# The last of 32 attention pairs turned in 32-row blocks, a one-column function at each change of ScalarE's table, and a new order of issue

## Chip, core and metric

One core of a Trainium2 chip runs the whole kernel. The metric is device time in microseconds (us) from launch to end, the median over several executions. Five engines run side by side, each with its own queue of instructions: TensorE (PE in the profile, with its weight loads as PEld), VectorE (DVE), ScalarE (ACT), GpSimd (POOL) and SyncE (SP), which only issues DMA transfers here.

## What is computed

Thresholded attention over 8 batches of 8 heads (576 tokens, head size 64), and behind it a gated MLP with a spatial gate. Cut to what matters:

```python
scores = scale * q @ k.T                                # 64 heads, 576 x 576
keep   = scores >= max(scores) - tau
attn   = where(keep, exp(scores - max(scores)), 0)
attn   = attn / (sum(attn) + 1e-9)
x      = heads_side_by_side(attn @ v)                   # (8, 576, 512)
h      = gelu_tanh(x @ w_in)                            # 512 -> 1024
u, v   = h[:, :512], h[:, 512:]
v_n    = (v - mean(v)) / sqrt(var(v) + 1e-6) * g_ln
v_s    = w_sg @ v_n + b_sg                              # mixes the 576 tokens
out    = x + (u * v_s) @ w_out
```

## The kernel before

**Attention.** The 64 heads are worked off as 32 pairs, four to a batch. A pair has nine score tiles: four of 128 query rows for each of its two heads, and one tile in which the last 64 rows of both heads share the partitions. A tile goes through a fixed sequence: scores on TensorE (L546, split into a rounded part and a remainder; L524 for the first four pairs), row maximum on VectorE (`nm`, L555), the threshold on GpSimd (`thr`, L561), the exponential on ScalarE (L582), and on VectorE the selection with the row sum (L589).

What then happens to the exponentials has two forms. In pairs 4 to 30 (`by_rows` is true) VectorE turns each tile in blocks of 32 x 32 (`turn_blocks`, L599), and TensorE multiplies them with the values in 288 small products of 32 rows (`turned_values`, L755), in up to six pieces. The values come in a layout that is repeated four times over the partitions, in four loads. The inverse row sums leave as one small transpose (`turn_rows`, L242), are copied by ScalarE (`take_rows`, L655), written to DRAM by three small DMAs (`put_rows`) and read back, spread over the partitions, by two (`get_rows`). VectorE then scales the result (`scale_turned`, L762, two halves).

In pairs 0 to 3 and in pair 31, the last, the form is the older one: TensorE turns the exponentials with whole 128 x 128 transposes (L242), ScalarE copies them from PSUM (L715, L730), and the value product (`values`, L741) follows in two parts, tokens 0 to 255 and 256 to 575. The inverse sums are repeated by GpSimd, turned by TensorE and copied by ScalarE, without DRAM.

Either way ScalarE rounds the result to `xh` (L780) and GpSimd takes the remainder `xl` (L785). These two are the input of the MLP.

**MLP.** A batch's MLP is cut into units of 8 to 14 products (L849): `v` units (moving width 512), `u` units, gate units `y` and output units `o` (width 288, or 256 and 320 in the last batch). A `v` unit runs over the four pairs of its batch; the last four of its twelve products need the batch's fourth pair. `v` and `u` units pass through gelu on ScalarE (L838). ScalarE holds one table of functions at a time: exp and gelu stand in two tables, and each change costs an ACT_TABLE_LOAD.

**Order.** Every step is first put into a list, `plan`. A table of numbers that is packed as text (`ORDER`) says in which order the steps are issued to the engines, and a second one (`FIRST_BANKS`) which of the eight PSUM banks each step takes. Each engine works its own part of that order strictly in turn:

```python
    def issue(plan):
        with tc.manual_schedule():
            for i in order:
                plan[i].fn()
```

The tail of the program is the MLP of the last batch: nothing of its `v` and `u` units can be finished before pair 31 is.

Of the kernel before, what the change touches and what calls it, by code (L numbers as in the profile page):

```python
# [22 lines left out]
P = 128  # L23
# [14 lines left out]
    "mK)W70_1gFy$8G1J1PU%|V;ChK6psNPywt2jHbcFf4nEN;GbJyM;l-yi$J`zN^6)s-UTzw(N;V%g3tJK&)1R0B3zxpl2tkBx6FLH^p~>)akE+*ZvSc$8"
    "=2NMU6De$>h|k7(5jjzjKQ74K(6)3)B1@>@Q@w%)b3q!5m#Tgy!}vEQZ9Z-YBcm9ejVXrLIU~i#t@_L*ErrWlTvT6p+#p5>Q)7x%0k^^9WfSO+&9LYxp"
    "TRo}m_;qI0UCBgO@q`&)pqVtNj1V@irhN0jdxs(jdD9Glk|llsw{oNITgbykItw1Om~7DHiBa+L*x?xDKqU8Vd0b##>wY|EB;HlPeGDu@FzHtc+kwE>J"  # L40
    "#CZM$~Yp^NF?1af!?^93nL4mkQJEdH{2%a!Us1)bMF0gn=;K8*VsR)C9+5I2tptYM2e-Rghss;uFlZD>+L23gsjyeoEVygR%A%@g$g({HmWN)fa}tlj#"
    "$2OB}zT+s73-*NVY0k42Cqs@<nZq6FG9$(I%T_|3XE;}rSl!Lk?>zv5?>@QPvz7xfzj!mzL!VnS@f&&9+O=Z-%jNUqC%@mVo==LQ*gKR3%2{Jeuwzi1u"
    "d8fRKK!iG66W|S%-mqyWZlxU4fay#solc4&AEoQ{e)es)K;GPwZ*=MFf@f&1wLw?$BXAmPidF<Y#LqOr-Q$8w!r((ivfy@m~P&VgRgffC)eDLfmf;>?j"
    "f*7-Om^;RwB6#u(W)weFOoYOtKiqBwT56tCc!rsG7Nx?=kY(M7htb4SCK;3o=Zg51xNkE(JSGmtOp4#M!f+ZWggTXs#0u7!IWwom0^&k`?p~CGVmgp`h"
    "9r|3$%sC@QiO9}_guy-Kk-bBYzgy5it(OkOoN(9HIgApkO}a-aCw#(Gs}u(CWbRD7OJ^s+HD&Wvu|=>e!_VXG#KT_tCLW%NJQQ_7h;uANiwU5)1$R*g~"
    "Z=hpA4tQbI%G`(#+a13PdP~ylG-pn*6sv<%)5%Y(h~qVn7zrVo*4#30oS`SVBd`;HVKS>iETSCY(Qwn<il<xIS$wF2cjpm}wIL<%3*~n5{tZ6S1xd!=x"
    "Fd&5hv*`@>s;s+x!k!4Z5Q61ObzUn(NgB&jV|2ABLt<5?p#EX37#12VS`{1VE>m^gEa84>=&Cr2XaZ{O4@AEsPR#3u=yhMF0uCSakEh=fm5!y;#h+u@d"
    "2*lbpq6dW6O91b<gkZ5M#B4(Ltw9OnB5g>W^f=I!aFew-j+(;&JL)%!qglkiie<Q`zh>zK#ta1dyZT#{?5*~q3R#fEH;EtG14I;Q3!jr)5Qf`FuB#Ue?"
    "dnU7H=uCjS*NBl-Gar)RHM}c}QjsJPH!(1xj8&)9xaYA-Ces|JRnl3TAx1;vj4@MID*O@385c$=uNc9nz}N0*EWA+7EIk7dmlv8wwNtJATd62VUY1&0N"
    "uipKS1Z5OtsEFb#WO@Doke9XxA2PM(NGlDg&<F~m8HmBio7mF*RZ0H7FMP#T~s%+s<k^m6Vau^z01mMh6~6lYzhtZZq==neF?*%3*L1$h4)sGaz=(2;u"  # L50
    "ot<+g|w?PTiyv1<b<XqiB%|RpC}Q_eB;8^DG>47#Iq3z(80TgOtH)lM(E(8_F>=NhZkrP_D^E*)P*(bhW*hN~SyRglCQl-o@GwKG_X5V&PsSo=I+u=xj"
    "vz)D4Uhm(h7_lJKav{YOW5k1{|oo~(NKP1CBkdxKym7)qXr@PA_HX0zg?a0;kkQW9}<mu(x4^!H<})b1rE+<na>IW;eBdnj$M@V7T8+O~21&3IV7U7(b"
    "jhoAQEpl!<LsjQvxzu&cq{0*5U1b@g7il7#NyiP4seg^rL%|||b@y^20KL+gJw+-_YM|d1TH*{zQRa1u?9#rni0(-fO^eI#2%Y%03kzjNMSTd{9j(LV0"
    ")0LY}4Q^_QYKcBYzzLowziTP5{1B9zQ|lU{2Ub-;y0b!#=}_Zn(eB$8Ogr8&wT^Z<KD>zpsS7$@bCN)f><1zzyQ8gE@VaXH$^McqT}Z<>Pj^NjxffbVl"
    "ag2Fxsci8j5m_B*5<h~PbVDfeKDhncsjWvgWYP?dR<K+FWfazm814~h#VOJ@WiFm1)~-Hw{b2~9iO?Udjiy7j!tVjkuFE&{?@5%9DFw8tn-?7&YBU`^F"
    "lXRe@9v04o#k*x4wtFctU_Qcu&ZS*U0hyG;+1ektBeWZ&FSd{0wkMQzsw+@|`DZGHgqh8hVobX(^;*lw;@JJK=caOGVKC&52+Ir|kN1jIE-3^R;nTu5T"
    "NYVynB*{Ro`_P}=EgY4Bf%NbtynKYC=ibO>6lQji29<QL{P6n=C%rOpcWRt>+u%w7kx))&a&>$VlH73eY64G)6ti|MOp-iRfEEz{-CcMhDjbMlFg@0|k"
    "Z@vfbS>nd2&pc0hG8-wbXjQ{?PItAno_4YtnPWMt>v3@x<8e*<CEl*hR@)8m`ch!y9mN%cP|Li4a>s$5DgIA8tJ=nb>E_U|EA&}PqTm<`)7dHSDz&G<?"
    "J>1ih`EltR0E^$G8`%A1d&3WpEqe?;anD~qA3l9?>_30#Esx(Zo)#={cs@P@&PO1LyfFXm7e76G6l4p?H{uF5mkjhp>JOI`O@OaR)0K%Zycrx&*5eaRb"
    "uV(kW=ogaOejgOeQa5elHMTauL;awn>HLGewwUmpn&$eyYFyV-P#N8Tb!GJ#BUp^0{CE`Mh2{&w{i|GcqRjOz%xzI2<+3?<G0BThkJAY`1y7KT{$!uU@"  # L60
    "5@+-y9lzD2dd(6uoic7b+qf1F&z@u6tqKR8;y#mm{BlPd|1m!#q6jfu&$Oozx2_ww>>l0##$boUZS={pay1XXApfVutd4w_(3QUJ-`((ZW8#sFq;N$0V"
    "m>LPV7BE0_}VOGz(gCUA!1xyjn=r0fJa1#09BSUXc*50F@&>VN?dI&K;LKRJ7c?8+gT0BHafhwWtaevcj}xa&P;m!{}SYwNB_U-uzFB5P`j0#JEVDJ07"
# [37 lines left out]
FIRST_BANKS = (  # L100
    "c-l3RO9I3&2ttkVbN?I9gLJyEO+^Gv1W(pPoV*o7$Q!3Jc<VGy<N#_iIbFg6Juw?+g;AmcY@S<frX1H^D(iI4DM8LS2XjTgmU(8c`n_&XMbTxdDXAg0g"
    "y}R60s5xJl5w+gfKfbZ<pZB*b+E|zlCu_@k}a1}EtjQ_gcdQ7_6>s-<-%=RUG#g2EAdzo-mm`j=j<nww(Hp(9cxepN&s?(JeMwL)Bw=1fwz?G<3w3}!p"
    "UuX>?%Qw+j!z5Ta^7b5N}qk-rMyrvr&jRvk=uhz5d%?!_+M=LJD;wMho$Dw9NblCgn<#ZFxFx%<^!an|&0om1^sTN30>$dIxJVd~Mo+i3p1kE)I~@NF+"
    "n@bw6(>T;N!g<g<88#}A9<2vh"
# [1060 lines left out]
```

## Time and profile before

| | |
|---|---|
| median of 3 runs | 906.46 us (905.97 to 910.84) |
| profiled execution, its own time | 908.68 us |
| its span, first to last instruction | 906.9 us |
| TensorE busy | 852.6 us, 94% |
| VectorE busy | 702.9 us, 78% |
| ScalarE busy | 601.4 us, 66% |
| GpSimd busy | 588.3 us, 65% |
| ACT_TABLE_LOAD | 100, 1283 ns each |

The profiled execution took 2.22 us more than the median, and 1.78 us of it lie outside the span. Busy TensorE time counts overlapping products once, so that the rest of the span, 54.3 us, is time without any product in flight.

### The profile page before, as it was taken

What the parts mean: (1) busy time and instruction counts of PE and PEld (TensorE: products, weight loads), DVE (VectorE), ACT (ScalarE), POOL (GpSimd) and SP (SyncE); (2) the same over time, 40 slices, a digit from 0 to 9 for tenths busy, and PEclk for the clock granted to TensorE, in tenths of its full rate; (3) what the DMA queues carried; (4) which work ended last, traced back from release to release, by engine and by line L of the source; (5) the groups of instructions that cost most, each with busy time, mean ns of one, the idle gap of its engine ahead of it and who ended that gap; (6) DMA issues with size and microseconds to landing.
All of it is one profiled execution on the core that took longest, in us unless ns stands there. A gap on an engine that the chain in (4) does not pass through costs nothing.

```text
span 906.9 us, 30418 instructions
## 1 busy us (share of the span) xinstructions
PE 852.6 (94%) x12440; PEld 752.9 (83%) x12440; DVE 702.9 (78%) x1436; ACT 601.4 (66%) x985; POOL 588.3 (65%) x973
## 2 busy tenths in 40 slices
...
GB/s 213 228 84 99 118 86 84 170 184 130 127 107 143 156 168 125 157 170 170 116 102 138 142 169 144 90 175 146 134 136 151 97 177 110 162 86 23 27 8 59
DMA packets 71998, 115.79 MB, mean 128 GB/s; under 512 B 10033, under 2 KB 32049, under 8 KB 71858
## 3 DMA queue, kind: packets, MB, share of 16 engines
...
q14 instruction: 42, 0.34, 0.1%
...
## 4 chain that ended last, share of the span: by engine, by line
PE 45%; DVE 18%; POOL 12%; ACT 10%; issue 8%; DMA 5%; SPq 2%; POOLq 0%; DVEq 0%; ACTq 0%
PE all_banks L849 26%; PE all_banks L546 8%; DVE nm L555 6%; DVE p L589 5%; PE all_banks L755 4%; DVE turned L599 4%; ACT p L582 3%; PE all_banks L242 2%; POOL ot L1056 2%; PE all_banks L741 2%; POOL vv L950 2%; PE all_banks L524 1%; POOL klz L448 1%; ACT L838 1%; POOL z L963 1%
## 5 line engine op out<-in xcount | busy, mean ns | idle before, releaser
L582 ACT ACTIVATE p<-all_banks,nm 128x576 f32<-128x576 f32 x256 | 184.5, 741 | 111.4 <-DVE nm L555 109.8
L589 DVE SCALAR_TENSOR_TENSOR p<-all_banks,nm,p 128x576 f32<-128x576 f32 x256 | 202.4, 808 | 51.7 <-ACT p L582 30.8
L555 DVE TENSOR_REDUCE nm<-all_banks 128x1 f32<-128x576 f32 x288 | 207.7, 742 | 34.6 <-PE all_banks L546 23.9
L546 PE MATMUL all_banks<-ks,qst 128*128 128x288 f32 x560 | 166.1, 316 | 19.1 <-DVE p L589 7.4
L599 DVE STREAM_TRANSPOSE turned<-p 128x576 f32<-128x576 f32 x216 | 159.1, 755 | 3.3 <-PE all_banks L755 3.2
L546 PE MATMUL all_banks<-klz,qst 128*128 128x288 f32 x560 | 156.8, 298 | 1.6 <-POOL klz L448 1.5
L561 POOL TENSOR_TENSOR nm<-columns,nm 128x1 f32<-128x1 f32 x288 | 53.3, 192 | 150.9 <-DVE nm L555 130.5
L755 PE MATMUL all_banks<-turned,v 32*64 32x144 f32 x7776 | 142.3, 286 | 3.8 <-issue 2.5
L755 PEld LDWEIGHTS all_banks<-turned,v 32*64 32x64 f32 x7776 | 123.1, 130 | 17.6 <-issue 13.8
L546 PEld LDWEIGHTS all_banks<-ks,qst 128*128 128x128 f32 x560 | 106.4, 190 | 36.6 <-DVE p L589 16.8
L849 PE MATMUL all_banks<-wsh,z 128*128 128x288 f32 (+2 forms) x512 | 114.1, 302 | 3.2 <-DVE pm L589 2.6
L546 PEld LDWEIGHTS all_banks<-klz,qst 128*128 128x128 f32 x560 | 106.8, 191 | 4.9 <-POOL klz L448 3.0
L849 PEld LDWEIGHTS all_banks<-wsh,z 128*128 128x128 f32 x512 | 86.5, 192 | 5.5 <-DVE pm L589 3.2
L448 POOL TENSOR_TENSOR klz<-rk,khi 64x576 fp32r<-64x576 f32 (+1 forms) x56 | 80.0, 1428 | 14.9 <-PE all_banks L546 5.6
L849 PE MATMUL all_banks<-gh,woh 128*128 128x288 f32 (+2 forms) x256 | 76.9, 303 | 2.7 <-DVE ir L762 1.3
L849 PE MATMUL all_banks<-xh,wih 128*128 128x288 f32 (+2 forms) x256 | 75.2, 298 | 2.1 <-DVE p L589 2.1
L849 PE MATMUL all_banks<-xh,wil 128*128 128x288 f32 (+2 forms) x256 | 74.1, 296 | 2.6 <-issue 2.6
L849 PE MATMUL all_banks<-wsl,z 128*128 128x288 f32 (+2 forms) x256 | 75.8, 300 | 0.0
L849 PE MATMUL all_banks<-gh,wol 128*128 128x288 f32 (+2 forms) x256 | 75.3, 297 | 0.0
L849 PE MATMUL all_banks<-xl,wih 128*128 128x288 f32 (+2 forms) x256 | 74.6, 296 | 0.0
L849 PE MATMUL all_banks<-gl,woh 128*128 128x288 f32 (+1 forms) x240 | 71.4, 299 | 1.8 <-issue 1.8
L838 ACT ACT_TABLE_LOAD x50 | 64.2, 1283 | 12.4 <-PE all_banks L849 10.8
...
## 6 DMA issues: line engine op xcount, KB each, us to landing
...
```

Of the source, the lines that this page charges most:

```text
L242: nc.tensor.transpose(out, x, ident_r.bitcast(F32))
L448: nc.gpsimd.tensor_tensor(klz[h][rows, 0:w], st["k"][rows, o:o + w], st["kh"][rows, o:o + w], ALU.subtract)
L546: nc.tensor.matmul(sc[:, a, 0:HALF], w, x, start=(j == 0), stop=(j == len(terms) - 1))
L555: nc.vector.tensor_reduce(nmax, st["s", h, i][:, :, 0:HALF], AX.XY, ALU.max, negate=True)
L561: nc.gpsimd.tensor_tensor(thr, toff, st["nm", h, i], ALU.subtract)
L582: nc.scalar.activation(target(h, i), st["s", h, i][:, :, 0:HALF], AF.Exp, bias=st["nm", h, i])
L589: nc.vector.scalar_tensor_tensor(dst, st["s", h, i][:, :, 0:HALF], st["thr", h, i], dst, ALU.is_ge, ALU.mult, accum_out=st["l"][:, c:c + 1])
L599: nc.vector.transpose(st["turned"][:, :, o:o + Q], st["p", i][:, c0:c0 + S].rearrange("p (k x) -> p k x", x=Q))
L741: nc.tensor.matmul(acc[h * D:(h + 1) * D, 0:w], st["v"][:, o:o + D], unit(h, a)[:, kt, 0:w] if kt < NM else tail_unit(a)[:, 0:w], start=(k ...
L755: nc.tensor.matmul(st["accs"][g // 2][hs, g % 2, 0:W], st["v"][rows, o:o + D], st["turned"][rows, k, h * W:(h + 1) * W], start=(k == 0), s ...
L838: put("gelu", end, lambda: nc.scalar.activation(tile_of(), acc_of(), AF.Gelu_apprx_tanh))
L849: nc.tensor.matmul(st["acc"], *term(j), start=(j == 0), stop=(j == n - 1))
```

## The change

Three things change. First, pair 31 takes the block-turned form of the pairs in front of it; the host side lays out its queries, keys and values accordingly. Second, wherever the order goes over from exp to gelu or back, a ScalarE function of one column (on a constant, into a column that nobody reads) is issued just ahead of the first function of the new kind. Third, the table `ORDER` and the table `FIRST_BANKS` are new.

```diff
 ORDER = (
-    "c-mE133wCL7M?R{?o65{Z7HQKZCSctX$uGxq#*bN!6%zg5J8`Spnxdiz96`M`rMw%Q)J%+!39*1@(=_!6j@3UC`)%*3bX}E(lp6T(%g6My)$V|!(`^(v"
+    "c-m!H31Ade((bP(^Li#TnVf{&90`G3gi}O7@IVlOH7trQt{@1=t|wmjdoAdyxazO02!<QnT}2KNqH=gcI2E}AxgaDYBq8Tq-AShZcXZFh{c}urzgP8D)"
...
     columns = cpool.tile([P, 4], F32, name="columns")
+    spare = cpool.tile([P, 1], F32, name="spare")
...
-        parts = SPLIT if whole_s or n == B * HP - 1 else ((0, S),)
+        parts = SPLIT if whole_s else ((0, S),)
         by_rows = len(parts) == 1
...
-    issue(plan)
+    issue(plan, {kind: partial(nc.scalar.activation, spare, mhalf, f)
+                 for kind, f in (("exp", AF.Exp), ("gelu", AF.Gelu_apprx_tanh))})
...
-    pairs = [divmod(n, h // 2) for n in range(WHOLE_SCORES, b * h // 2 - 1)]
+    pairs = [divmod(n, h // 2) for n in range(WHOLE_SCORES, b * h // 2)]
...
-    def issue(plan):
+    def issue(plan, tables):
+        ready = None
         with tc.manual_schedule():
             for i in order:
+                kind = plan[i].kind
+                if kind in tables and kind != ready:
+                    if ready:
+                        tables[kind]()
+                    ready = kind
                 plan[i].fn()
```

Over the whole program TensorE keeps its 32 pairs' scores and all MLP products. The program before holds 100 table loads, 50 ahead of exp and 50 ahead of gelu; the changed one holds 90, one at the start and 89 ahead of the one-column functions.

**TensorE at the last pair, before.** These rows stand where pair 31's product with the values is made. The tiles `p` and `pm` hold exponentials, `ir` and `l` inverse sums, `pt` the turned exponentials, `rv` the values; rows on `wol` and `woh` are `o` units of batch 6. Row by row, a count at the end means so many products of that kind in turn.

```order
L849 MATMUL all_banks<-gh_0_1_12135,wol_123 128x288
L242 MATMUL all_banks<-ident_r,p_2_12519 128x128 x5
L242 MATMUL all_banks<-ident_r,p_3_12573 128x128 x5
L242 MATMUL all_banks<-ident_r,pm 128x128 x4
L242 MATMUL all_banks<-ident_r,p_3_12573 128x128 x4
L724 MATMUL all_banks<-both,pm 128x64
L242 MATMUL all_banks<-ident_r,ir_12583 128x128 x2
L242 MATMUL all_banks<-ident_r,l_12140 128x128
L741 MATMUL all_banks<-pt_0_12498,rv_2576 64x256 x10
L741 MATMUL all_banks<-pt_1_12569,rv_2576 64x320 x10
L849 MATMUL all_banks<-gh_1_0_12621,woh_116 128x288
L849 MATMUL all_banks<-gl_1_0_12627,woh_116 128x288
```

Eighteen whole transposes, the inverse sums and both parts of the value product stand in one block; the `o` units of batch 6 come behind it.

**TensorE at the last pair, changed.** The same place. `turned` holds the exponentials after VectorE's block turns, `v_31` the repeated values; a count of 96 on such a row stands for two thirds of the 288 small products.

```order
L242 MATMUL all_banks<-ident_r,ir_12644 65x128
L849 MATMUL all_banks<-gh_1_0_12662,woh_117 128x288
L849 MATMUL all_banks<-gl_1_0_12690,woh_117 128x288
L849 MATMUL all_banks<-gh_1_0_12662,wol_121 128x288
L849 MATMUL all_banks<-gh_1_0_12662,woh_118 128x288
L849 MATMUL all_banks<-gh_1_0_12662,woh_117 128x288
L849 MATMUL all_banks<-gl_1_0_12690,woh_117 128x288
L849 MATMUL all_banks<-gh_1_0_12662,wol_121 128x288
L849 MATMUL all_banks<-gh_1_0_12662,woh_118 128x288
L755 MATMUL all_banks<-turned_12522,v_31_12580 64x144 x96
```

The one transpose of the inverse sums comes first, eight products of `o` units follow, then two thirds of the small products. Another 20 products of `o` units stand between these and the last third, and 16 more behind it.

**ScalarE at a change of table, before.** This is the second half of batch 0's `u` units (`uu0_1`), with what each row waits for in brackets.

```order
L582 ACTIVATE p6_0_1854<-all_banks_93,nm6_1_0_1861 128x576 [waits DVE_49]
L838 ACT_TABLE_LOAD [waits PE_49]
L838 ACTIVATE uu0_1_0_1897<-all_banks_93 128x288 [waits Activation_49]
L838 ACTIVATE uu0_1_1_1899<-all_banks_93 128x288 [waits Pool_49]
L1053 ACTIVATE ot0_0_0_1901<-all_banks_93 128x288 [waits PE_49]
L655 ACTIVATE ir5_1895<-all_banks_93 9x128 [waits PE_49]
L838 ACTIVATE uu0_1_2_1909<-all_banks_93 128x288
L582 ACT_TABLE_LOAD
L582 ACTIVATE p6_1_1920<-all_banks_93,nm6_0_1_1918 128x576 [waits DVE_49]
```

The load ahead of gelu carries the wait for TensorE, the load ahead of exp carries none.

**ScalarE at the same place, changed.**

```order
L582 ACTIVATE p6_0_1848<-all_banks_93,nm6_0_0_1846 128x576 [waits DVE_49]
L1164 ACT_TABLE_LOAD
L1164 ACTIVATE spare_106<-columns_105 128x1 [waits Activation_49]
L838 ACTIVATE uu0_1_2_1900<-all_banks_93 128x288 [waits Pool_49]
L838 ACTIVATE uu0_1_1_1902<-all_banks_93 128x288 [waits PE_49,Pool_49]
L439 ACTIVATE qhi7_1904<-rq7_1730 128x640 [waits DMAHW4_49,DMAHW5_49,DMAHW3_49,DMAHW2_49]
L838 ACTIVATE uu0_1_0_1906<-all_banks_93 128x288
L1053 ACTIVATE ot0_0_0_1908<-all_banks_93 128x288 [waits PE_49]
L655 ACTIVATE ir5_1876<-all_banks_93 9x128 [waits DMAHW1_49,PE_49]
L1164 ACT_TABLE_LOAD
L1164 ACTIVATE spare_106<-columns_105 128x1 [waits Activation_49]
L582 ACTIVATE p6_1_1930<-all_banks_93,nm6_0_1_1927 128x576 [waits DVE_49]
```

Each load now stands ahead of a one-column function that waits for nothing but an earlier one of its kind; the wait for the MLP products has gone to the gelu behind it.

**VectorE at the last pair, changed.** Names as above; `uu` are gate products of batch 6 and `nm` row maxima.

```order
L555 TENSOR_REDUCE nm_0_3_12609<-all_banks 128x1
L555 TENSOR_REDUCE nm_1_3_12617<-all_banks 128x1
L589 SCALAR_TENSOR_TENSOR p_3_12611,l_12223<-all_banks,nm_1_3_12617,p_3_12611 128x576
L599 STREAM_TRANSPOSE turned_12522<-p_2_12541 128x18x32
L589 SCALAR_TENSOR_TENSOR p_3_12611,l_12223<-all_banks,nm_0_3_12609,p_3_12611 128x576
L599 STREAM_TRANSPOSE turned_12522<-p_3_12611 128x18x32
L1003 TENSOR_TENSOR uu_1_2_12345<-all_banks,uu_1_2_12345 128x288
L625 RECIPROCAL ir_12644<-l_12223 128x9
L1003 TENSOR_TENSOR uu_1_3_12665<-all_banks,uu_1_3_12665 128x288
L599 STREAM_TRANSPOSE turned_12522<-p_3_12611 128x18x32
L762 TENSOR_TENSOR ir_12644<-all_banks,ir_12644 128x288 x2
```

The rows on `turned` are new here (nine in all for the pair), and the scaling by `ir`, two rows of width 288, takes the place of one row each of width 320 and 256.

## Rows read from the trace of the kernel before

**Rows 1.** The page: span, busy time by engine, the chain that ended last.

```profile
span 906.9 us, 30418 instructions
...
PE 852.6 (94%) x12440; PEld 752.9 (83%) x12440; DVE 702.9 (78%) x1436; ACT 601.4 (66%) x985; POOL 588.3 (65%) x973
...
PE 45%; DVE 18%; POOL 12%; ACT 10%; issue 8%; DMA 5%; SPq 2%; POOLq 0%; DVEq 0%; ACTq 0%
PE all_banks L849 26%; PE all_banks L546 8%; DVE nm L555 6%; DVE p L589 5%; PE all_banks L755 4%; DVE turned L599 4%; ACT p L582 3%; PE all_banks L242 2%; POOL ot L1056 2%; PE all_banks L741 2%; POOL vv L950 2%; PE all_banks L524 1%; POOL klz L448 1%; ACT L838 1%; POOL z L963 1%
```

**Rows 2.** Windows: stretch, length, busy us of PE, PEld, DVE, ACT, POOL, PEclk.

```profile
200.00:300.00 100.00, 88.78 (x1573) 80.43 (x1572) 81.14 (x164) 60.59 (x90) 58.90 (x98) 0.95 0.48 131
300.00:400.00 100.00, 98.55 (x1680) 91.29 (x1679) 87.78 (x176) 73.60 (x112) 69.39 (x111) 1.00 0.54 150
...
sum 700.00, PE 660.83 PEld 600.72 DVE 586.38 ACT 471.77 POOL 461.30; mean PE 94.40 PEld 85.82 DVE 83.77 ACT 67.40 POOL 65.90
```

**Rows 3.** Windows around the last pair's end and after it.

```profile
820.00:843.00 23.00, 23.00 (x309) 20.20 (x308) 10.55 (x25) 12.35 (x31) 10.33 (x21) 1.00 0.09 28
843.00:907.00 64.00, 60.05 (x410) 57.35 (x409) 8.99 (x21) 23.41 (x48) 42.91 (x58) 1.00 0.08 29
```

**Rows 4.** Timeline, last pair on TensorE: start us, length us, what.

```profile
835.19 1.25 PE L242 MATMUL all_banks<-ident_r,p 128*128 128x128 f32 x10
...
836.28 0.60 PE L242 MATMUL all_banks<-ident_r,pm 128*128 128x128 f32 x4
...
837.75 5.07 PE L741 MATMUL all_banks<-pt,rv 128*64 128x256 f32 x40
...
842.75 0.40 PE L849 MATMUL all_banks<-gh,woh 128*128 128x288 f32 x1
```

**Rows 5.** Timeline of TensorE alone, from 771 to 783 us.

```profile
771.97 0.39 PE L849 MATMUL all_banks<-wih,xh 128*128 128x512 f32 x1
...
774.70 0.29 PE L849 MATMUL all_banks<-xh,wih 128*128 128x288 f32 x1
...
775.22 0.29 PE L546 MATMUL all_banks<-ks,qst 128*128 128x288 f32 x1
...
779.63 3.62 PE L755 MATMUL all_banks<-turned,v 32*64 32x144 f32 x192
783.19 0.40 PE L546 MATMUL all_banks<-ks,qst 128*128 128x288 f32 x1
```

**Rows 6.** Groups by line and shape: busy us, mean ns, idle time ahead.

```profile
L599 DVE STREAM_TRANSPOSE turned<-p 128x576 f32<-128x576 f32 x216 | 159.1, 755 | 3.3 <-PE all_banks L755 3.2
...
L582 ACT ACT_TABLE_LOAD x50 | 64.2, 1283 | 3.7 <-DVE nm L555 2.1 <-PEq L1146 0.7
L838 ACT ACT_TABLE_LOAD x50 | 64.2, 1283 | 12.4 <-PE all_banks L849 10.8 <-DVE vt L909 0.8
...
L785 POOL TENSOR_TENSOR xl<-ir,xh 128x576 fp32r<-128x576 f32 x27 | 38.7, 1434 | 10.2 <-ACT xh L780 10.1
...
L780 ACT ACTIVATE xh<-ir 128x576 fp32r<-128x576 f32 x27 | 18.4, 681 | 14.6 <-DVE ir L762 10.6 <-POOL ot L1056 2.1 <-issue 1.6
...
L680 ACT ACTIVATE ir<-all_banks 64x64 f32<-64x64 f32 x10 | 2.2, 218 | 0.1
```

**Rows 7.** Timeline of ScalarE, one change of function table.

```profile
606.36 1.28 ACT L838 ACT_TABLE_LOAD   x1 [2.44 <-PE all_banks L849]
607.65 0.41 ACT L838 ACTIVATE uu<-all_banks 128x288 f32<-128x288 f32 x1
```

**Rows 8.** Timeline, pair 11: its inverse sums leave TensorE and come back.

```profile
308.54 0.27 PE L242 MATMUL all_banks<-ident_r,ir 128*65 128x128 f32 x1
...
316.82 0.82 DVE L762 TENSOR_TENSOR ir<-all_banks,ir 128x288 f32<-128x288 f32 x2
```

**Rows 9.** Timeline, the same two steps of pair 30.

```profile
813.06 0.27 PE L242 MATMUL all_banks<-ident_r,ir 128*65 128x128 f32 x1
...
825.06 0.82 DVE L762 TENSOR_TENSOR ir<-all_banks,ir 128x288 f32<-128x288 f32 x2
```

More of the change, by code (lines that the diff above doesn't have):

```diff
@@ L38 @@
[L38 to L62, printed above, removed]
@@ new lines @@
+    "mK&Ty&g%@*{?2zex-oKesumPne*m=Zcd5^HfO2?#ISBmNP18rgd~NYbr>j26~cu6|CP{%0K2CWR4O#jE&)T#bcdtp?4oyzfO{7J`;{mLy_Y!x9neFFFh"
+    "rO-^T%*iAWFitjsVAGniBVkYk;Fl0V90V3dadZ%!-L2yk@3!{={V@K`9R&CPM;`N=lGIyqUwCa|R<Bfk51HX$FW;o&>#|DK^bW(1Q$0T!m6=QV>i9CyU"
+    "K>69vyPvlVc7CA%bfdEm^Ya5oiYBUIGR=Dh6BYg{ES$K>-yqS-$c6kbw6kIa3v8`jv2odM7rs?J0ik2W^I$9y_>z{F)&FIA?tB%k1!VF}(i7?<GoI0Ti"
+    "G+zxNBj+qyd?xk4XF6bg3cEKMr!WF#YQ<7|Mnd5LDxOZmkA!nFj20*>?*+kq%I)dF{WXR6^uzQ0!7M6735qCfe0@#I>ZY^pz?wD&dREonuC{a2G)g_yc"
+    "{o5FxPeAHEQ2{o3M`wJxiD>t-$B=V&pW&;GJ^3UyM<po5lG(6=egn`T(#9`7gMJ%T3<l4P8SuK<?{t(QNQO@gJXG%Hx@6;M+&gaA<`bTnYmSc__VF?1D"
@@ new lines @@
+    "zn6+rUO1ME%bcc1ix^%*sxCuDl-kH!T|-kO*dHJGCT&(62oQsoEDpqH^?zb&;<{sQ-(O7@(DzPZ(+zxM9_-K0e6K5VES#u&mV<tI?wNd{lzmb`9cf}0N"
+    "p4F9<bCcHIfueyy1eOsr!QKzRjRd;sohNHrPc8;rK$UG%pxdIR4=FL5CE{Pyd4Z0Ta_D#f;Vr)L>GCWn=O|4}+VNE-HgnIEz#dvQP0OroyRK{JN1dojM"
+    "ZYMxgkDH6ZaYs5sU2DW*lLV)HXVziu<dBre10mAEZmx6T&*!n{)a^oHsxOrK%vG;-Zfl{p{6MV;yU%}tC63vzURQMfdV#*kncv-uShB*>V~#r({Q-)JE"
+    "EB=m(3EJgfY(Sz-)`=!u^&HUlkLR&}oZC^2BVFJ407k5(en>z|Ku5+pkaYf=r{dx#YOz{CfXOh<rBZmF!It5^;e1;)15Ro;>aLwQ|ctYXq_(eQilS}gO"
+    "b%S@qk{OG_CyWpbADD5!aTel$X3)YH<_MSa2UjmcSu#W6+0!{GY+j^@r%*DIV?uHxevx5wg%eJQ;xcj}xaGCxHv;3_vJqXC2+y=hu@tNozhZbq@pxX%6"
@@ new lines @@
+    "69=1Vp=Th{@^03E5UJHxW%;@d8(*O$!~;0Z;0Pmv`lil9}CT+Bni5~>CuB#!wX(GMt`W7pQuL9>O#_BP!BR@kgSV>Pzn1m1pNl{Dv^TDh_LA=ca*RgLM"
+    "<<X6M)1B%BUm1s4*r%)NY4S#R!)w=z;)AQWe!~K%yG!kwjQpm>%^;r4I_tlQ1V}WCC2uSiR^iqe&$?hwHYDGC?kEq*!=Ponp$ITBfO*g2Z?hW(g-p*da"
+    "_=6}CCgT!a|fA_6YRj51MO0I)dJ(6q>?xfrNCy}~`BG6y;R0+gt~JEH{mm*8352s*gVaL1YJf^s5pd(3fef#C&LDPrQNq4k!BBj6Z_WEP*QcXLEy85OF"
+    "+OT(s_LPLXxL1nBwB2_X1l?++k1P(5Zx=EzSE8*Ga1gb_Fc)+?KHbl4pCPr@flbBRZheS*Q*DMJU7%L|+Nkj<{=D1NDy5TD^EE3Tflqc25G%o>R$)F;{"
+    "CyRhrj8!rNq4Qd(1cC)-zS0qmpX3CHQAvbP8<lD(7=Canc$%mMty_XZ?1XB?s&+dI3L#z=#Hb7&B6ZIYGz^=CE3#`el&)Jt{jW0PX6{3EN;E5f&{zRzR"
```

93 lines of the change are left out of this document (51 added, 42 removed).

## Prediction

> **What bounds the kernel now.** I read the page first, then the windows, then the timeline around the last pair, and the groups by line for prices. The page puts TensorE at 852.6 us of a span of 906.9 us; VectorE follows with 702.9 us, ScalarE with 601.4 us [rows 1]. The chain that ended last runs over TensorE for 45% and over VectorE for 18%, with ScalarE at 10% [rows 1]. So TensorE sets the time, and what a change is worth is TensorE's work that it removes plus the pauses of TensorE that it closes or opens; 54.3 us of the span are pauses.
>
> The windows show where those stand. In the seven stretches of 100 us from 100 to 800 us TensorE was busy for 660.83 of 700 us, which leaves 39.2 us of pauses, 5.6 us for each [rows 2]. They are uneven: the best stretch lost 100 - 98.55 = 1.45 us, the worst 100 - 88.78 = 11.2 us, and in the worst the granted clock averaged 0.95, so that it fell to the lower of its two levels (1.2 of 2.4 GHz) for about a tenth of the stretch [rows 2]. These stretches do the same kind of work, so the difference is a matter of order. Around the end of the last pair, from 820 to 843 us, TensorE was busy all 23.00 us at a clock of 1.00, with VectorE at 10.55 us; behind it 60.05 of 64 us [rows 3]. Work taken off TensorE there comes off the end, unless something new is late.
>
> **The last pair on TensorE.** Removed are 45 transposes: 36 for nine tiles, four for the tails, five for the inverse sums. Ten of them take 836.28 - 835.19 = 1.09 us, 0.109 us each, so 45 take 4.9 us [rows 4]. The old value product fills 842.75 - 837.75 = 5.0 us [rows 4]. Added are 288 small products: 192 fill 783.19 - 779.63 = 3.56 us, so 288 take 5.3 us [rows 5], and one transpose of 0.1 us. Scores stay. The balance is 4.9 + 5.0 - 5.3 - 0.1 = **4.5 us less**. Starts are subtracted from starts, so the cost of going from one shape to another is in the 3.56 us.
>
> The Trainium skill, in "TensorEngine Tiling (Array Packing)", section "Key Properties", says that a change of tiling mode drains TensorE, which speaks against small products in two more pieces. It gives no price; a drain of one whole 0.29 us product at each of four changes would take 1.2 us of the 4.5 and put the sum below at 902.2 instead of 901.0.
>
> **What lies beside it.** VectorE gets nine block turns at 755 ns, 6.8 us [rows 6]. I count them at nothing: from 820 to 843 us VectorE was idle for 12.4 us [rows 3]. Without that cover they cost up to 6.8 us. ScalarE loses the copies out of PSUM, which were off the path. SyncE gets four loads of values for one, and five small DMAs. The value buffer is free once pair 30's last product has run; between that and pair 31's first small product the new order has 120 MLP and score products at 0.13 us [rows 5], 16 us. The other pairs load the same four under an equal reuse, so I count this at nothing too.
>
> The inverse sums now go through DRAM. From the transpose to the scaling this took 316.82 - 308.54 = 8.3 us in pair 11 and 825.06 - 813.06 = 12.0 us in pair 30 [rows 8, 9]. In the new order TensorE has, behind that transpose, eight products of 0.13 us, 192 small ones (3.56 us), 20 products and the last 96 (1.8 us): 1.1 + 3.6 + 2.7 + 1.8 = 9.1 us. After 8.3 us the sums are there in time. Then come the scaling (0.82 us), `xh` (0.68 us) and `xl` (1.43 us) [rows 6, 8], 2.9 us; against them stand 16 products (2.1 us), and twelve products of width 512 that do not yet need this pair, at (774.70 - 771.97) / 12 = 0.23 us each [rows 5], 2.7 us. The cover is 4.8 us. With 8.3 us nothing is late. With 12.0 us `xl` is ready 14.9 us after the transpose and the cover ends at 13.9 us: 1.0 us lost. I take nothing, since pair 30's 12.0 us held a wait for its own products, and keep 1.0 us for the range.
>
> **The table changes.** A load takes 1283 ns, before exp as before gelu [rows 6]. Ten fewer are 12.8 us less on ScalarE. No function of one column is in this trace; the smallest one, 64 x 64, takes 218 ns [rows 6], so 89 take 19.4 us. Net, ScalarE works 6.6 us more; at its 10% of the chain [rows 1] that is 0.7 us. From the other side: most loads already start without waiting (the 50 gelu loads have 12.4 us of idle time ahead of them, the 50 exp loads 3.7 us) [rows 6], and those that waited are what the one-column function can bring forward, as the load that stood 2.44 us behind TensorE and pushed its gelu by 1.28 us [rows 7]. The gelu loads hold 1% of the chain [rows 1], 9 us of their 64.2 us, or 14%; 14% of the 12.4 us is 1.7 us. I take 0.7 - 1.7 = **1.0 us less**. The bounds are 9 us less (every gelu load leaves the path) and 6.6 us more (ScalarE binds all along); the first asks for idle time ahead of each load, which is not there, and the second for an engine that is not at 66%.
>
> On this price the Trainium skill differs: "ScalarE: Activation LUTs", section "What ACT_TABLE_LOAD costs", adds about 1380 ns of drain to the load, 2.66 us a change. Ten fewer would then be 26.6 us, ScalarE's net 7.2 us less, and the forecast 899.6 us. The trace does not agree here: the gelu begins 0.01 us after the load ends [rows 7].
>
> **The new order** is the part without a row. All steps are issued in another sequence from the first DMA on. I take its pauses as equal, 0, with a bound from the stretches: one like the worst made average gains 11.2 - 5.6 = 5.6 us, and up to 5 us of clock (0.05 of 100 us); one average made like the worst loses as much.
>
> **Sum.** Against its own time the profiled execution goes from 908.68 to 908.68 - 4.5 - 1.0 = 903.2 us (1.8 us of it outside the span). It lay 2.2 us above the median, so the median is forecast at 906.46 - 5.5 = **901.0 us**. One measurement of this kernel can tell about 0.5%, 4.5 us, from no change: faster means below 901.9 us, slower above 911.0 us. The forecast stands close to the first of these.
>
> **The rivals.**
>
> *The forecast*, 901.0 us, own range 897 to 905: 0.42, a little over half of it (0.23) below 901.9 us.
>
> *The new order also closes pauses.* For it: the stretch from 200 to 300 us, 11.2 us and a fallen clock, has much to give, and neighbours do the same work with 1.45 us [rows 2]. Against it: the order keeps the pace of the old one, pair by pair. One such stretch made average gives 901.0 - 5.6 = 895.4 us, with its clock 890: 0.29.
>
> *VectorE becomes the bound at the last pair.* The nine turns come between maxima and selections that free the PSUM banks of the scores, and the inverse sums wait for the last selection. For it: VectorE holds 18% of the chain [rows 1]. Against it: the 12.4 us of idle time [rows 3]. With all 6.8 us on the path, 907.8 us: 0.15. The saving is then not seen in the time.
>
> *Slower: the new order opens a stretch like the worst one.* A place in the steady part, where the MLP's products stand behind a score tile whose bank VectorE has not freed, costs 5.6 us over the average and 5 us of clock, 10.6 us: 911.6 us; from the best stretch 9.8 + 5 = 14.8 us, 915.8 us. It decides from 10.0 us on (5.5 gained and 4.5 that can be told). For it: one such stretch exists [rows 2]. Against it: six of seven are better. 0.14.
>
> **Numbers.** Faster 0.23 + 0.29 = 0.52; same 0.19 + 0.15 = 0.34; slower 0.14. The range reaches down to the second case with its clock, 890, and up to the lower price of the last, 912.
>
> **What would show it.** L741's rows for pair 31 gone and 8064 small products in place of 7776; behind the last of them no pause of TensorE over 0.5 us ahead of the `v` units; the scaling of pair 31 8 to 12 us after its transpose; 90 table loads; one-column functions near 0.22 us; the gelu behind each with no load in between. TensorE busy near 848 us. Wrong would be: a pause of several microseconds ahead of the last `v` units (the chain through DRAM), or pauses in the seven stretches that sum to something far from 39 us, which would make the order of issue, and not the last pair, the main term.

## The result, and the profile after

The changed kernel takes 881.78 us (median of four runs, 880.13 to 884.55) where the one before takes 906.22 us: ratio 0.9727, 95% interval 0.9678 to 0.9775, some 24.7 us less. Forecast were 901.0 us, range 890 to 912, so the sign was right and the size was not: the gain is more than four times the 5.5 us of the sum. The profiled execution took 880.19 us, 1.6 us below the median, where that of the kernel before lay 2.5 us above its own: the traces differ by 28.5 us, the medians by some 24. One execution of 1450.83 us (run old_order_new_pair, granted clock 0.765) is left out of that run's ratio; its median below counts it.

The page of the kernel after, for the lines of [rows 1]:

```profile
span 878.4 us, 30879 instructions
PE 841.2 (96%) x12642; PEld 745.7 (85%) x12642; DVE 707.3 (81%) x1444; ACT 592.6 (67%) x1045; POOL 585.6 (67%) x965
PE 46%; POOL 13%; DVE 8%; ACT 5%; issue 5%; DMA 5%; SPq 1%; POOLq 0%; DVEq 0%; ACTq 0%
```

TensorE is still the bound. What shrank in the chain is VectorE, from 18% to 8%, and ScalarE, from 10% to 5%, while VectorE's busy time went up: what TensorE lost by waiting for them got less, not their work. The windows, for [rows 2]:

```profile
200.00:300.00 100.00, 93.47 (x1618) 83.19 (x1616) 84.28 (x170) 67.24 (x112) 59.51 (x99) 1.00 0.51 139
300.00:400.00 100.00, 97.63 (x1665) 89.84 (x1665) 85.68 (x171) 73.83 (x122) 69.33 (x112) 1.00 0.55 145
sum 700.00, PE 677.34 PEld 617.25 DVE 600.11 ACT 481.31 POOL 468.34; mean PE 96.76 PEld 88.18 DVE 85.73 ACT 68.76 POOL 66.91
```

In the seven stretches TensorE now pauses for 700 - 677.3 = 22.7 us instead of 39.2. The worst stretch is 4.7 us better and its clock is back at 1.00; the best is a little worse. Over the whole execution, between TensorE's first and last product, the time without any product fell from 48.8 to 31.7 us (the gaps of all product rows summed), 17.1 us. (The 54.3 us that the prediction calls pauses hold 5.5 us more, ahead of the first product and behind the last.) TensorE's busy time fell by 852.6 - 841.2 = 11.4 us, and 17.1 + 11.4 are the 28.5 us of span. In the busy time lie the clock and the removed work. The mean granted clock rose from 0.987 to 0.996. At the lower of the two levels products of width 288 start 0.24 us apart instead of 0.13 (rows in the last section), about half the work in a stretch, so the clock cost some (1 - 0.987) x 906.9 = 11.8 us before and 0.004 x 878.4 = 3.5 us after: an estimate of 8.3 us. With the 4.5 us of removed work that is 12.8 us for the 11.4 us measured: pauses first, clock second, work third. The clock of one execution is not that of the next: those of the kernel after had 0.988 to 0.996, and the slowest of them, 884.55 us, had the lowest.

The groups by line and shape for [rows 6], and ScalarE's timeline for [rows 7]:

```profile
L755 PE MATMUL all_banks<-turned,v 32*64 32x144 f32 x8064 | 147.1, 286 | 2.7 <-issue 1.7 <-ACT uu L838 0.4 <-DMA v<-in_vR 0.3
L1164 ACT ACT_TABLE_LOAD x89 | 114.2, 1283 | 1.6
L1164 ACT ACTIVATE spare<-columns 128x1 f32<-128x1 f32 x89 | 18.1, 203 | 1.0
```
```profile
599.11 1.28 ACT L1164 ACT_TABLE_LOAD   x1
600.41 0.20 ACT L1164 ACTIVATE spare<-columns 128x1 f32<-128x1 f32 x1
600.52 0.39 ACT L838 ACTIVATE uu<-all_banks 128x288 f32<-128x288 f32 x1
```

The loads now stand in front of a function that waits for nothing: all 89 together had 1.6 us of idle time ahead, where the gelu loads alone had 12.4.

### The profile page after: what moved, and what is told of

Its sections match the earlier page's. It is cut to its first block, busy times and chain, and to the rows that moved or that the text cites. A ratio compares the mean times of both kernels' runs of the same rounds, so it can differ in the third digit from the quotient of the medians.

```text
span 878.4 us, 30879 instructions
## 1 busy us (share of the span) xinstructions
PE 841.2 (96%) x12642; PEld 745.7 (85%) x12642; DVE 707.3 (81%) x1444; ACT 592.6 (67%) x1045; POOL 585.6 (67%) x965
## 4 chain that ended last, share of the span: by engine, by line
PE 46%; POOL 13%; DVE 8%; ACT 5%; issue 5%; DMA 5%; SPq 1%; POOLq 0%; DVEq 0%; ACTq 0%
PE all_banks L849 29%; PE all_banks L546 9%; PE all_banks L755 7%; POOL ot L1056 3%; DVE nm L555 2%; DVE turned L599 2%; DVE p L589 2%; POOL klz L448 2%; ACT L1164 2%; DMA v<-in_vR 1%; POOL gl L1023 1%; POOL rq L465 1%; ACT p L582 1%; POOL vv L950 1%; POOL nm L561 1%
## 5 line engine op out<-in xcount | busy, mean ns | idle before, releaser
L546 PE MATMUL all_banks<-ks,qst 128*128 128x288 f32 x560 | 164.2, 312 | 12.5 <-DVE p L589 7.4
L599 DVE STREAM_TRANSPOSE turned<-p 128x576 f32<-128x576 f32 x224 | 165.6, 756 | 2.2 <-PE all_banks L755 2.1
L755 PE MATMUL all_banks<-turned,v 32*64 32x144 f32 x8064 | 147.1, 286 | 2.7 <-issue 1.7
L755 PEld LDWEIGHTS all_banks<-turned,v 32*64 32x64 f32 x8064 | 127.5, 130 | 16.3 <-issue 11.9
L1164 ACT ACT_TABLE_LOAD x89 | 114.2, 1283 | 1.6
L849 PE MATMUL all_banks<-wsh,z 128*128 128x288 f32 (+2 forms) x512 | 110.7, 298 | 0.6 <-DVE p L589 0.6
L448 POOL TENSOR_TENSOR klz<-rk,khi 64x576 fp32r<-64x576 f32 x56 | 79.9, 1427 | 15.4 <-PE all_banks L546 8.4
L849 PEld LDWEIGHTS all_banks<-wsh,z 128*128 128x128 f32 x512 | 84.0, 188 | 2.7 <-DVE p L589 1.1
L849 PE MATMUL all_banks<-wsl,z 128*128 128x288 f32 (+2 forms) x256 | 73.9, 296 | 0.0
```

The source lines that it names most:

```text
L448: nc.gpsimd.tensor_tensor(klz[h][rows, 0:w], st["k"][rows, o:o + w], st["kh"][rows, o:o + w], ALU.subtract)
L546: nc.tensor.matmul(sc[:, a, 0:HALF], w, x, start=(j == 0), stop=(j == len(terms) - 1))
L599: nc.vector.transpose(st["turned"][:, :, o:o + Q], st["p", i][:, c0:c0 + S].rearrange("p (k x) -> p k x", x=Q))
L755: nc.tensor.matmul(st["accs"][g // 2][hs, g % 2, 0:W], st["v"][rows, o:o + D], st["turned"][rows, k, h * W:(h + 1) * W], start=(k == 0), s ...
L849: nc.tensor.matmul(st["acc"], *term(j), start=(j == 0), stop=(j == n - 1))
L1164: tables[kind]()
```

## The experiments

Ratios are to the kernel before, run beside each; a difference of two runs is the difference of their ratios times 906.5 us, and its 95% interval reaches 3 to 6 us to either side. "Pauses" are worked out as above, the clock is the mean granted one; both are of the profiled execution alone, which can lie off the median: that of only_ahead_of_exp took 897.48 us, the slowest of five, and the other four had clocks of 0.990 to 0.994.

| run | median us | ratio (95%) | pauses us | clock |
|---|---|---|---|---|
| after | 881.78 | 0.9727 (0.9678 to 0.9775) | 31.7 | 0.996 |
| no_onecol | 888.94 | 0.9791 (0.9745 to 0.9837) | 35.4 | 0.993 |
| old_order_onecol | 901.38 | 0.9935 (0.9907 to 0.9962) | 42.7 | 0.990 |
| old_order_new_pair | 911.0 | 1.0048 (1.0019 to 1.0076) | 55.3 | 0.986 |
| old_order_both | 907.3 | 0.9995 (0.9967 to 1.0023) | 48.1 | 0.983 |
| new_to_pair8 | 906.14 | 0.9990 (0.9963 to 1.0016) | 47.3 | 0.980 |
| new_to_pair16 | 904.43 | 0.9972 (0.9949 to 0.9995) | 45.4 | 0.985 |
| old_to_pair8 | 887.81 | 0.9800 (0.9767 to 0.9833) | 38.6 | 0.992 |
| old_to_pair16 | 885.96 | 0.9770 (0.9731 to 0.9809) | 36.2 | 0.990 |
| old_to_pair30 | 896.94 | 0.9906 (0.9876 to 0.9936) | 41.3 | 0.981 |
| new_pair16_to_20 | 902.41 | 0.9946 (0.9922 to 0.9970) | 49.8 | 0.991 |
| only_ahead_of_gelu | 881.14 | 0.9729 (0.9696 to 0.9761) | 31.9 | 0.994 |
| only_ahead_of_exp | 891.89 | 0.9843 (0.9806 to 0.9879) | 38.6 | 0.984 |
| one_column_twice | 887.44 | 0.9772 (0.9739 to 0.9806) | 34.5 | 0.990 |
| banks_again | 950.34 | 1.0480 (1.0444 to 1.0516) | 77.3 | 0.972 |
| new_order_ruled_banks | 904.6 | 0.9976 (0.9954 to 0.9999) | 46.9 | 0.988 |
| old_order_ruled_banks | 915.7 | 1.0111 (1.0071 to 1.0151) | 56.6 | 0.985 |
| new_order_fitted_banks | 881.92 | 0.9710 (0.9673 to 0.9747) | 32.1 | 0.988 |
| fitted_only_gelu | 881.0 | 0.9712 (0.9680 to 0.9744) | 31.9 | 0.994 |

**The three parts one by one.** The first run is the new kernel without its one-column functions; the other three keep the old order and bank table and put in one part or both. There the block-turned pair takes the places of the old form's steps.

```diff
 # no_onecol: the new kernel, less this
-                if kind in tables and kind != ready:
-                    if ready:
-                        tables[kind]()
-                    ready = kind
                 plan[i].fn()
...
 # old_order_onecol: the same lines added to the kernel before
...
 # old_order_new_pair, old_order_both: the new kernel's plan, in the old order
-    order, banks = table()
+    order, banks = old_order_mapped_to_the_new_plan, old_banks
```

> The changed kernel with its order, bank table and last pair, but without the 89 one-column functions; the loads stand ahead of exp and gelu again, 90 of them. If the order of issue brought the gain, it stays near 882 to 886 us. If the one-column functions brought it, most goes: 895 to 902 us.

> The kernel before, its order and last pair kept, with a one-column function at each of its 99 changes of table. If the order brought the gain: 904 to 908 us. If the one-column functions did: 888 to 895 us.

> The old order and old banks, only pair 31 in the block-turned form, its new steps put where its old ones stood. By the forecast's term for the last pair: 4.5 us off, 901 to 902 us. If the last pair is worth more than its products (a rival for the missing 20 us): 885 to 895 us.

> The old order with the block-turned last pair and the one-column functions: all of the change but the new order. If the order is the main part: 899 to 903 us, about 20 us over the changed kernel. If the two others work together: 882 to 888 us.

None of the four came out within a range expected for it: the first two lie between their two theories, the last pair made the kernel slower instead of faster, and the last run lies above both of its ranges.

The one-column functions are worth 0.0064 x 906.5 = 5.8 us in the new order, 5.9 us in the old with the old pair and 4.8 us with the new pair. The second alone is clear of noise against the kernel before (0.9907 to 0.9962); that all three agree speaks for the others. In the old order no load is saved (100 loads before and with them), so this is not the ten loads but the waiting of the others. The last pair, in the places of the old form, makes the kernel 4.4 us slower (2 to 7). And the two parts together leave the old order where it was, 0.9995: the new order and its bank table bring the remaining 0.0268 x 906.5 = 24.3 us (19 to 29).

Why the last pair costs time in the old places: the window from 800 to 870 us in the kernel before and in old_order_new_pair, and TensorE's timeline in the latter (in brackets the wait ahead of a row and what ended it).

```profile
800.00:870.00 70.00, 69.91 (x744) 64.22 (x743) 26.07 (x57) 36.42 (x71) 37.93 (x65) 1.00 0.12 38
```
```profile
800.00:870.00 70.00, 63.79 (x909) 58.84 (x908) 30.30 (x62) 28.12 (x48) 32.20 (x52) 0.95 0.18 59
```
```profile
824.67 0.40 PE L545 MATMUL all_banks<-ks,qst 128*128 128x288 f32 x1 [1.60 <-DVE ir L761]
...
834.50 0.33 PE L241 MATMUL all_banks<-ident_r,ir 128*65 128x128 f32 x1 [0.81 <-DVE ir L624]
837.65 4.79 PE L754 MATMUL all_banks<-turned,v 32*64 32x144 f32 x127 [2.02 <-DVE turned L598]
```

TensorE stands at the scores, at the inverse sums and at the first small product, each time for VectorE, 6.0 of the 6.2 us of pauses in this window, where the kernel before had 0.1 us, and the granted clock averages 0.95 instead of 1.00, some 3.5 us more by the estimate above. Against 4.5 us of removed work that makes about 5 us slower; 4.4 were measured. In the new places the same work has no gap; windows of the run old_to_pair30 and timeline of TensorE in the kernel after:

```profile
800.00:870.00 70.00, 70.00 (x979) 65.77 (x979) 28.41 (x58) 30.56 (x58) 40.21 (x61) 1.00 0.16 49
```
```profile
808.78 0.27 PE L242 MATMUL all_banks<-ident_r,ir 128*65 128x128 f32 x1
...
810.23 3.25 PE L755 MATMUL all_banks<-turned,v 32*64 32x144 f32 x192
813.41 0.40 PE L849 MATMUL all_banks<-gl,woh 128*128 128x288 f32 x1
...
816.26 1.78 PE L755 MATMUL all_banks<-turned,v 32*64 32x144 f32 x96
817.97 0.40 PE L849 MATMUL all_banks<-gl,woh 128*128 128x288 f32 x1
...
825.42 0.39 PE L849 MATMUL all_banks<-wih,xh 128*128 128x512 f32 x1
```

**Where the order gains.** The plan's steps were taken in one order up to a cut and the rest in the other, each with its own bank numbers. Near the cuts both orders have issued the same steps but for two to four.

```python
head  = first[:cut]          # pair 8: 1121, pair 16: 2192 or 2235, pair 30: 4010 of 4658
order = head + [step for step in second if step not in head]
# new_pair16_to_20: old[:2235], then new up to place 2795, then old
```

> The new kernel's work and one-column functions; steps in the new order up to the start of pair 8's scores, in the old order behind it (the last pair block-turned, in the old form's places), so it lies between the old order with both other parts (907.3 us) and the new kernel (881.8 us). By the pauses of TensorE in those two traces: spread theory, the gain sits in all of the order: 3 us of pauses and 1 us of clock come from this first quarter, 903 us. One-place theory, the gain is the bad stretch from 240 to 270 us with its clock and the last pair's places: neither is in this part, 907 us.

> As above with the cut in pair 16, at about half of the time. Spread theory: the second quarter adds 3 us of pauses and 3 us of clock to the first, 897 us. One-place theory: the stretch from 240 to 270 us is now in the new order, 5.6 us of pauses and 5 us of clock, 896 us, and all of it comes between the run with the cut at pair 8 and this one (11 us where the spread theory has 6).

> The reverse of the first: old order up to the start of pair 8's scores, the new one behind it. Spread theory: 4 us are lost against the new kernel, 886 us. One-place theory: the stretch from 240 to 270 us and the last pair are in the new order, 882 us, as the new kernel.

> The old order up to the end of pair 30's loads and the new one behind it, with both other parts: only the places of the last pair are new. The old places cost 6.2 us of pauses between 820 and 838 us and about 1 us of clock. If the places of the last pair are all that was wrong in that stretch, 900 us; 4.5 us below that of the old order with the old last pair and the one-column functions (901.4 us) would be 896.9 us. If VectorE is too late whatever the place, 907 us. If nearly all of the order's gain is here, under 890 us.

> The old order up to pair 16, order and banks of the new kernel behind it, both other parts. If the gains of the stretches add up (1.2 us up to pair 8, 1.7 to pair 16, 12.2 to pair 30, 10.4 behind it), 881.8 + 2.9 = 884.7 us. If what the new order does in its first half is needed for the second (to pair 8 it was worth 6.0 us seen from the new kernel, 1.2 seen from the old order), 888 us or more.

> The old order with both other parts (907.3 us), but the steps from pair 16 to pair 20 in the new order. In the old order this window holds a pause of 2.0 us for a late block turn near 523 us, 0.7 to 1.0 us behind it, and a granted clock of 0.93 from 500 to 550 and 0.97 from 450 to 500 us. Local theory: pauses and clock are made by the places inside the window, so these four pairs alone give back 4 us of pauses and 5 us of clock: 898 us. Carried theory: what the new order gains there was prepared in the pairs before (a lead of the scores that builds up), so the window alone gives 2 us or less: 905 to 907 us.

Spread and one-place theory each hit once at most. At the cut in pair 8 the time is near the one-place theory's 907 us (906.1), with the first eight pairs old near the spread theory's 886 (887.8); at the cut in pair 16 both miss (897 and 896, measured 904.4). With only the last places new the time is the 896.9 us of the last pair's 4.5 us; the run old_to_pair16 (886.0) lies between its two ranges.

From the old order with both parts (0.9995) to the kernel after: new places from pair 30 on give 0.9995 - 0.9906, 8.1 us; from pair 16 to pair 30 another 0.9906 - 0.9770, 12.3 us; ahead of pair 16 the last 0.0043, 3.9 us. The first two are clear of noise (4 to 12 and 8 to 17), the third is not (-2 to 10). One place it was not: the cut at pair 16 puts the bad stretch of [rows 2] into the new order and gives 0.9995 - 0.9972 = 2.1 us, not 11. That theory falls, and an even spread falls with it, since half of the order gave 2 us there. Whether the parts simply add is open: up to pair 8 the new order is worth 0.5 us seen from the old side and 6.6 us seen from the new, and the intervals (-3 to 4 and 1 to 12) overlap.

The window from 500 to 550 us, in the old order there (old_to_pair30) and in the new (old_to_pair16):

```profile
500.00:550.00 50.00, 46.45 (x716) 42.50 (x715) 41.50 (x83) 29.39 (x50) 30.59 (x52) 0.93 0.54 152
```
```profile
500.00:550.00 50.00, 49.15 (x819) 43.45 (x818) 42.41 (x87) 29.34 (x52) 34.92 (x58) 1.00 0.62 168
```

2.7 us of pauses and 0.07 x 50 = 3.5 us of clock come from one 50 us window, and 819 products run there instead of 716. With only pairs 16 to 20 in the new order the clock was 1.00 from 450 to 600 us as well, and the pauses there fell by 2.5 us, near what the local theory asked for. But the run gained 4.4 us (1 to 8) and not its 9: from 400 to 450 us the pauses rose from 0.9 to 3.0 us (the kernel after has 2.8 there too), and from 600 to 800 us by 2.2 us. So part of what is gained inside the window is paid outside it. The carried theory's 2 us lie within the interval; how much is local and how much carried stays open.

**Order or bank table.** The old and the new table have 175 of 704 numbers in common, a quarter. Three other tables were put under the orders.

```python
free = [b for b in banks if the place in the order allows it]
bank = min(free, key=place_of_last_reader)              # banks_again
bank = min(free, key=end_of_last_reader)                # ruled, from pair 3 on
bank = max((b for b in free if end_of_last_reader(b) <= start_of_product),
           key=end_of_last_reader)                      # fitted, from pair 3 on
```

> The new kernel with its order and one-column functions; of its 704 bank numbers, 498 are another: each product takes, among the banks free at its place in the order, the one free the longest. Order theory: the order decides when a bank is needed, and any table that is free at that place serves: 880 to 885 us. Bank table theory: the numbers are part of the 25.5 us, since a product that gets a bank just freed stands until VectorE has read it: 890 us or more.

> The new kernel's order and one-column functions; from pair 3 on the banks follow one rule, the same in the next run: of the banks free at a place, the one whose last reader ended first in the trace of the kernel with this order (a bank whose partner is free too counts as 3 us later). 474 of 704 numbers are others than in the new table. Order theory: with one rule for both orders the new one stays 20 to 26 us faster, 882 to 888 us here. Bank table theory: the old and the new table are what differs, and with one rule for both the orders come out within 8 us of each other, both between 890 and 905 us.

> The old order with the block-turned last pair and the one-column functions, and from pair 3 on banks by the same rule, from the trace of the kernel with this order; 492 of 704 numbers are others than in the old table. Order theory: 905 to 912 us. Bank table theory: 890 to 905 us, near the run above.

> The new kernel's order and one-column functions; from pair 3 on the banks follow another rule: of the banks free at a place, the one whose last reader ended latest but still ahead of the product's start, both read from the new kernel's trace, so that banks free early are left to those that need them early. 456 of 704 numbers are others than in the new table. Put beside the times of the trace, 11 products would find their bank late, by 2.0 us in all (the rule of the earliest reader: 36 products, 24.5 us; the table of 950 us: 65 products, 78.2 us). If late banks are all that a table does, 881 to 885 us; if the numbers matter in another way, or lateness in one trace says nothing of another table, near the 904.6 us of the earliest reader.

> As the last, with the one-column functions only ahead of gelu. A candidate for the fastest: 44 functions of 0.203 us less on ScalarE are at most 8.9 us of work off an engine that holds 5% of the chain, 0.4 us: 881 to 884 us.

A bad table costs the new order 68 us, the common rule 23 us, and the fitted one nothing: 0.9710 against 0.9727. The order theory's 880 to 885 us for any free table is refuted by the first. Counted beforehand from the new kernel's trace, the fitted table had 2.0 us of late banks, and the other two, counted after their runs, 24.5 and 78.2 us; measured are nothing, 22.6 and 68.3 us. So the new numbers as such bring nothing; what counts is how late the banks are. Under the common rule the two orders are 1.0111 - 0.9976, 12.2 us apart (8 to 16): neither the order theory's 20 to 26 us nor the 8 us of the bank table theory. Without the one-column functions ahead of exp the fitted table gives the same (0.9712). TensorE's waits in new_order_ruled_banks, in banks_again and in new_order_fitted_banks (us in total, times, longest); the first row of each is the scores' wait for VectorE's selection, which all three have:

```profile
PE all_banks L544 <- DVE p L587: 6.9, 16, 1.1
PE all_banks L847 <- DVE uu L1001: 6.5, 5, 1.6
PE all_banks L847 <- ACT ot L1051: 4.6, 3, 2.5
PE all_banks L847 <- ACT uu L836: 2.2, 4, 0.6
```
```profile
PE all_banks L544 <- DVE p L587: 6.6, 16, 0.9
PE all_banks L847 <- DVE uu L1001: 12.9, 8, 2.8
PE all_banks L847 <- ACT uu L836: 12.4, 8, 4.9
```
```profile
PE all_banks L544 <- DVE p L587: 9.9, 20, 1.1
PE all_banks L544 <- ACT uu L836: 1.1, 1, 1.1
PE all_banks L847 <- ACT uu L836: 0.2, 1, 0.2
```

The rows on L847 are MLP products that stand until VectorE's gate product or ScalarE's gelu or output copy has read the bank that they were given. With the fitted table next to nothing is left of them. No such table was made for the old order, so what the best table would give the old order, and with it the split of the 24.3 us between order and table, stays open. The old table has such waits too, scores behind a scaling or the MLP's sum `vt`; the first two rows are of old_order_both, the third is of the kernel after, which has no wait for `vt`:

```profile
PE all_banks L545 <- DVE ir L761: 6.6, 6, 1.8
PE all_banks L545 <- DVE vt L908: 2.5, 1, 2.5
```
```profile
PE all_banks L546 <- DVE ir L762: 1.1, 3, 0.5
```

The difference, 8.0 us, is half of the 16.4 us by which the pauses of these two runs differ.

**The one-column functions.** Only one side, or two at each change:

```diff
-                    if ready:
+                    if ready and kind == "gelu":      # only_ahead_of_exp: "exp"
                         tables[kind]()
...
 # one_column_twice
                         tables[kind]()
+                        tables[kind]()
```

> The new kernel with the one-column functions only where gelu comes next; ahead of exp the load stands in front of the first exp again. Gelu theory: TensorE's products are ready late and the load stood behind them (TensorE waited 6.0 us for the gelus' results without any one-column function, 0.7 us with them), so all 7.2 us are kept: 882 us. Exp theory: the exps stand on VectorE's chain, and half or more is lost: 886 to 888 us.

> The counterpart: one-column functions only where exp comes next. Gelu theory: as with none, 889 us. Exp theory: 883 to 885 us. Both sides count: 885 to 886 us here and in the other.

> The new kernel with two one-column functions at each change of table, 89 x 0.203 = 18.1 us more work on ScalarE (66% busy). Cheap theory: ScalarE's share of the chain is 5%, 0.9 us: 882.7 us. Dear theory: what ScalarE does between a load and its first function is on the path of gelus and exps, half or more of it counts: 891 us or more.

Ahead of gelu alone they are worth as much as on both sides (0.9729), ahead of exp alone nothing that can be told: 0.9843 (0.9806 to 0.9879), with none 0.9791 (0.9745 to 0.9837). The gelu theory holds. The gelu loads in no_onecol and in only_ahead_of_exp, the exp loads in only_ahead_of_gelu, and a wait of TensorE in only_ahead_of_exp and in only_ahead_of_gelu:

```profile
L836 ACT ACT_TABLE_LOAD x45 | 57.7, 1283 | 19.7 <-PE all_banks L847 14.2 <-DVE turned L597 2.7 <-DVE vt L907 2.2
```
```profile
L836 ACT ACT_TABLE_LOAD x45 | 57.7, 1283 | 19.4 <-PE all_banks L847 13.9 <-DVE turned L597 2.7 <-DVE vt L907 2.2
```
```profile
L580 ACT ACT_TABLE_LOAD x44 | 56.5, 1283 | 0.8
```
```profile
PE all_banks L544 <- ACT uu L836: 3.7, 4, 1.3
```
```profile
PE all_banks L544 <- ACT uu L836: 0.4, 1, 0.4
```

A gelu waits for TensorE's products, its load waited with it, and 1.28 us later than need be the bank came free, for which TensorE stood. All of TensorE's waits for gelus (`uu` and `vv`) together are 6.2 us in no_onecol, 6.4 in only_ahead_of_exp, 1.3 in only_ahead_of_gelu and 1.1 in the kernel after: 5.1 us less, for the 5.8 us of the functions. The exp loads wait for next to nothing, 0.8 us for all 44. The doubled functions put 18.1 us more on ScalarE and cost 0.0045 x 906.5 = 4 us; its interval leaves room from nothing to 9 us, so between the two theories this run does not decide.

## Why the prediction was wrong, by its own steps

**The step that failed** is "I take its pauses as equal, 0". The new order and its table are worth 24.3 us beside the other two parts, as much as the whole gain. I had the trace's 39.2 us of pauses in seven stretches before me, and the rival that the order closes some, but sized that rival by one stretch with its clock, 11 us. The runs show 12.3 us from pair 16 to 30 and 8.1 us behind it; ahead of pair 16, where the worst stretch lies, they show 3.9 us that is not clear of zero. What shrank is pauses (48.1 to 31.7 us from old_order_both to the kernel after) and with them the time at the lower clock (0.983 to 0.996). How much of it is order and how much table stays open.

**The last pair, -4.5 us.** TensorE's work was right: 288 small products took 813.41 - 810.23 = 3.18 and 817.97 - 816.26 = 1.71 us, 4.9 us for the 5.3 reckoned from [rows 5]. These times run from start to start and hold the changes of shape, so the 1.2 us that the prediction set against them for drains does not show. (All its busy time, 841.2 us where 848 were forecast, is lower by the clock too.) That it comes off the end is not true in the old places. There it costs 4.4 us: "VectorE becomes the bound at the last pair", the second rival (907.8 us), is what happens (910.9 by the ratio). With the new places from pair 30 on, the kernel with both parts stands 0.9935 - 0.9906 = 2.6 us below the one with the one-column functions alone; the intervals allow -1 to 6, which holds the 4.5. This difference also holds what the new places do for the other steps behind pair 30, which no run separates. Counting VectorE's nine turns at nothing by the 12.4 us of idle time [rows 3] was not enough: 7.2 of the 12.4 us lay behind the last selection, where VectorE waited for the old value product (the kernel before):

```profile
842.97 0.82 DVE L769 TENSOR_TENSOR ir<-all_banks,ir 128x320 f32<-128x320 f32 x2 [7.22 <-PE all_banks L741]
```

The turns have to be done before the small products that replace that product, so this idle time could not hide them: in the old places the first small product waited 2.02 us for a turn.

**The way through DRAM.** 819.52 - 808.78 = 10.74 us from transpose to scaling, within the bounds from [rows 8, 9], and TensorE had no pause over 0.5 us behind it, as forecast; VectorE's row:

```profile
819.52 0.82 DVE L762 TENSOR_TENSOR ir<-all_banks,ir 128x288 f32<-128x288 f32 x2 [9.76 <-DMA ir<-ld]
```

**The table changes, -1.0 us** measured -5 to -6. The side was right (gelu loads behind TensorE) and so was the price of a function, 203 ns for 218. The size was not: I took the loads' 1% of the chain as the share of their idle time that counts, 14% of 12.4 us. It was 5.9 us in the old order, 48% of the 12.4 us, and 5.8 us in the new one, where the gelu loads without a one-column function waited 14.2 us for TensorE (the row of no_onecol). What counted was TensorE's own wait for the gelus' banks, which the sum had no term for. Why the chain shows so little of it stays open. The other price in that term, 0.7 us for more work on ScalarE, no run measures closely: one_column_twice has 4 us (0 to 9) for 18.1 us of work.

On the drain that the Trainium skill states ("ScalarE: Activation LUTs", "What ACT_TABLE_LOAD costs"): after the load of 1283 ns the next function begins 0.02 us later here too. That the result lies nearer to the sum made with the drain (899.6 us) is no support for it.

**Pauses and clock.** "[P]auses in the seven stretches that sum to something far from 39 us" was named as the sign that the order is the main term; they sum to 22.7.
